# Order of the last slot-expert products, their part widths, and the last hidden slot in a fused attention and mixture-of-experts kernel

## The chip, the cores and the metric

The kernel runs on one core of one Trainium2 chip. The metric is the device time of one execution in microseconds. Three runs of the kernel before gave 500.28, 500.62 and 500.79 us; the median is 500.62. All data are float32 in memory.

## The reference

Three steps follow one another. Only the last one ends in the region of the change, but all three fix what it must compute.

```python
# attention: q, k, v (4, 8, 576, 64), p (4, 8, 32, 64)
p_packed = sm_attn(p, k, v)
x = sm_attn(q, p_packed, p_packed)        # -> (2304, 512)

# first mixture: 4 experts, w1 (512, 1024), w2 (1024, 512), probabilities per row
for e in range(4):
    h = np.maximum(x @ w1[e], 0.0)
    out += p[:, e:e + 1] * (h @ w2[e])
x = out

# second mixture: 8 experts with 4 slots each, m1 (512, 1024), m2 (1024, 512)
logits = x @ phi
d = softmax of logits over the rows
slot_input = (d.T @ x).reshape(8, 4, 512)
for e in range(8):
    h = np.maximum(slot_input[e] @ m1[e], 0.0)
    slot_out[e] = h @ m2[e]
c = softmax of logits over the slots
out = c @ slot_out.reshape(32, 512)       # (2304, 512)
```

## The kernel before, in words

**Main loop (L1057).** It runs over 128 slots `s`. A slot is 128 of an expert's hidden columns for one batch of 576 rows. `mm1(s)` (L614) multiplies on TensorE into two PSUM tiles `h`, one for each half of 288 rows. A half is evicted in one of two ways into `ht`: either ScalarE applies the relu (L637) and POOL (GpSimd) multiplies by the row's probability (L638), or VectorE does both in one instruction (L632). VectorE takes the second half of every odd slot, ScalarE with POOL the rest. `flip_h` (L643) then turns `ht` in blocks of 32 by 32 on VectorE into `hr` (L648); it is issued one slot later, ahead of the next slot's `mm1`. `logits` (L653) multiplies four slots' `ht` with `wphi` into `lg`, two PSUM banks.

**Between the loop and the stream.** After slot 127 the last `flip_h` and `logits` are issued, then the generator `softmaxes` (L689) is advanced step by step. Its first step copies `lg` to `la`, one half on ScalarE (L696) and one on VectorE (L697). Its second step sums over the four groups on TensorE (`lr`, L701) and reduces the result on VectorE (L707). The third step takes exponentials and turns them. `pooling` (L776) then multiplies the turned weights with `hr` into `pb` (L788).

**The stream.** From here on the matrices w2, m1 and m2 come in 80 chunks of 512 KB each (`chunks`, L821), all issued by SP in a fixed order (L863). A chunk goes to a slot of 128 by 1024 elements as soon as that slot is free: the slots are former buffers of the main loop, among them `wphi`, `work` and the regions of `hr`, which `pooling` sets free as it proceeds. TensorE works through the chunks in their order: products with w2 (`si`), with m1 (`hid`), and with m2 (`so`).

**m2 and the output.** `so_steps` (L816) lists 32 chunks of m2, each used by one turn of the loop at L1262. The products accumulate in one PSUM tile `so` of 512 columns. For the first five experts a chunk holds whole rows of 512 columns (two blocks of rows, four matmul records of 512 columns). The last three experts are cut into two column parts of 256 (`PARTS`): first all their chunks for columns 0 to 255, then all for columns 256 to 511. Such a chunk has four blocks of rows with 256 columns each (eight matmul records), and rows of 1 KB where a whole-width chunk has runs of 4 KB. When a part is complete, ScalarE copies it (L1282), TensorE sums over its four groups (`sr`, L1284), ScalarE changes the sign (`rr`, L1286), and 18 matmuls `o` (L1298) make the part's output in six tiles of three. The 18 results are evicted alternately by ScalarE and VectorE (`drain`, L1259), and SP stores each tile (L1305).

**What sets the order.** The program is written out by hand in this region: each engine executes its instructions in the order in which the code issues them. The `so` tile keeps one of six PSUM banks; `o` tiles rotate through the other five. A turn of the loop at L1262 that completes no part ends with `continue`, so the second part's products are issued after all of the first part's tiles.

Of the kernel before, what the change touches and what calls it, by code (L numbers as in the profile page):

```python
# [18 lines left out]
def tile_packed_attention_moe_softmoe(  # L19
# [21 lines left out]
    NB, H, S, D = q.shape  # L41
    NE, DM, DF = w1.shape
    NX = m1.shape[0]
# [6 lines left out]
    SPB = 4 * NCH  # L50
    NFT = DF // 128
# [3 lines left out]
    CHUNK = 1024  # L55
# [30 lines left out]
    def mm_ps(name, keep=False):  # L86
        i = min((i for i in range(6) if i not in kept), key=lambda i: idle_since[i])
        clock[0] += 1
        idle_since[i] = clock[0]
        t = bank(i, name)  # L90
        if keep:
            kept[i] = t
        return t
# [28 lines left out]
    def place(b, i):  # L122
        return (NE * b + i) % RING
# [488 lines left out]
    ht_t, hn_t, lg_t = {}, {}, {}  # L612

    def mm1(s):  # L614
        ci, kf = divmod(s, 4)
        b = ci // NCH
        gg = g_t[ci]
        pr = pe_t[ci // 2]
        ht = ht_pool.tile([128, S], F32, tag="ht", name=f"ht{s}")
        fs = slice(128 * kf, 128 * kf + 128)  # L620
        for r in range(2):
            ps = mm_ps(f"h{s}_{r}")
            ts = slice(HS * r, HS * r + HS)
            for g in range(2):
                ah, al = a2_t[b, g]
                for i, (l, m) in enumerate(((0, ah), (0, al), (1, ah))):
                    pe.matmul(  # L627
                        ps[:, :HS], gg[:, l, g, fs], m[:, ts],
                        start=(g == 0 and i == 0), stop=(g == 1 and i == 2),
                    )  # L630
            if r and kf % 2:
                dve.scalar_tensor_tensor(  # L632
                    out=ht[:, ts], in0=ps[:, :HS], scalar=0.0, in1=pr[:, ts],
                    op0=ALU.max, op1=ALU.mult,
                )
            else:
                act.activation(out=ht[:, ts], in_=ps[:, :HS], func=AF.Relu)  # L637
                pool.tensor_tensor(out=ht[:, ts], in0=ht[:, ts], in1=pr[:, ts], op=ALU.mult)  # L638
        ht_t[s] = ht
        if kf == 3:  # L640
            del g_t[ci]

    def flip_h(s):  # L643
        ci, kf = divmod(s, 4)
        b, ch = divmod(ci, NCH)
        i, hf = divmod(ch, 2)
        f0 = 32 * (4 * hf + kf)
        dve.transpose(  # L648
            out=hr[:, place(b, i), :, f0 : f0 + 32],
            in_=ht_t[s].rearrange("p (x t) -> p x t", t=32),  # L650
        )

    def logits(ci):  # L653
        b, ch = divmod(ci, NCH)
        e, hf = order[ci // 2], ci % 2
        if ch == 0:
            lg_t[b] = [bank(6 + r, f"lg{b}_{r}") for r in range(2)]
        for r in range(2):
            for x in range(4):
                pe.matmul(  # L660
                    lg_t[b][r][32 * x : 32 * x + 32, :HS],
                    wphi[:, NFT * e + 4 * hf + x, :],
                    ht_t[4 * ci + x][:, HS * r : HS * r + HS],
                    start=(ch == 0),
                    stop=(ch == NCH - 1),
                    tile_position=(0, 32 * x),
                )
        for x in range(4):
            del ht_t[4 * ci + x]
# [141 lines left out]
    parts, d0 = [], 0  # L811
# [1 line left out]
        parts.append((d0, dw))  # L813
        d0 += dw

    so_steps = [(i, x, 0, DM) for i in range(NX - 3) for x in range(0, NFT, CHUNK // DM)]  # L816
    for d0, dw in parts:
        so_steps += [
            (i, x, d0, dw) for i in range(NX - 3, NX) for x in range(0, NFT, CHUNK // dw)
        ]  # L820
    chunks = []  # L821
    for x in range(0, NFT, 2):
# [19 lines left out]
    def add_slots(n, make):  # L842

        group = []
        for i in range(n):
            slots.append((make, n, i, group))
# [47 lines left out]
    def leftover(p, n, k=0):  # L894
        return flat[p][:, left + k : left + k + n]
# [4 lines left out]
    with tc.manual_schedule():  # L900
# [118 lines left out]
        nslot = NB * SPB  # L1019
# [6 lines left out]
        sg = {}  # L1026
# [29 lines left out]

        for s in range(nslot):  # L1057
            ci, kf = divmod(s, 4)
            if s:
                flip_h(s - 1)  # L1060
            mm1(s)
            if kf == 0:
                if ci + 1 < NB * NCH:
                    for _ in make_g(ci + 1):
                        pass
                if ci:
                    while wphi_done[0] < min(ci, NCH):
                        next(wgen, None)
                    logits(ci - 1)
            if s < SPB:  # L1070
                for _ in range(2):
                    next(wgen, None)
            for f in todo.pop(s, []):
                f()
            for gen in list(att_gens):
                if next(gen, "end") == "end":
                    att_gens.remove(gen)
            last = s - (NB - 1) * SPB
            if last == 0:
                att.close()  # L1080
                open_stream("s1", "right")
                for _ in range(2):
                    add_slots(1, a2_place)
            elif last == 8:
                hr_slots([place(NB, 0)])
                fold = leftover(place(NB, 0), 64)
                pool.tensor_tensor(
                    out=fold.rearrange("p (a s) -> p a s", a=2),
                    in0=ident.rearrange("p (a b s) -> p a b s", a=2, b=2)[:, :, 0],
                    in1=ident.rearrange("p (a b s) -> p a b s", a=2, b=2)[:, :, 1],  # L1090
                    op=ALU.add,
                )
            elif last == SPB - 5:
                add_slots(2, w1_place)
                add_work(0)
                add_work(1)
            if last >= 0:
                fill_stream(1)
# [6 lines left out]


        b = NB - 1
        flip_h(nslot - 1)
        logits(NB * NCH - 1)
        sg[b] = softmaxes(b, True)  # L1110
        for _ in range(2):
            next(sg[b])
        wp = mm_ps("idle")
        for _ in range(20):
            pe.transpose(wp[:, :128], ident, ident)
# [47 lines left out]
        ck = 0  # L1163
# [95 lines left out]
            (act.copy if tn[0] % 2 else dve.tensor_copy)(dst, src)  # L1259

        so = mm_ps("so", keep=True)
        for n, (i, x, d0, dw) in enumerate(so_steps):  # L1262

            nx = CHUNK // dw
            t = chunk_t.pop(ck)
            ck += 1
            for xl in range(nx):
                c = (nx * n + xl) % 4
                pe.matmul(  # L1269
                    so[32 * c : 32 * c + 32, d0 : d0 + dw],  # L1270
                    hm[:, x + xl, 32 * i : 32 * i + 32],
                    t[:, dw * xl : dw * xl + dw],
                    start=(nx * n + xl < 4),
                    stop=(dw < DM and i == NX - 1 and x + nx == NFT),
                    skip_group_check=True,
                    tile_position=(0, 32 * c),
                )
            load_chunk()
            if dw == DM or i < NX - 1 or x + nx < NFT:
                continue  # L1280
            so_sb = leftover(1, dw, d0)
            act.copy(so_sb, so[:, d0 : d0 + dw])  # L1282
            sr = mm_ps(f"sr{d0}")
            pe.matmul(sr[:, :dw], rep, so_sb, start=True, stop=True)  # L1284
            rr = end[:, CHUNK : CHUNK + dw]
            act.mul(rr, sr[:, :dw], -1.0)  # L1286
            for b2 in range(NB // 2):
                rows = out[2 * b2 * S : 2 * (b2 + 1) * S, d0 : d0 + dw].rearrange(
                    "(r x) d -> r x d", x=XR
                )  # L1290
                cv = ct[:, b2].rearrange("p x b r t -> p x (b r t)")
                for j0 in range(0, XR, nt):
                    jn = min(XR - j0, nt)
                    ob = out_tile()
                    ps = [mm_ps(f"o{d0}_{b2}_{j0}_{j}", keep=True) for j in range(jn)]
                    for j in range(jn):
                        o = slice(32 * j, 32 * j + 32)
                        pe.matmul(  # L1298
                            ps[j][:, :dw], cv[o, j0 + j], rr[o], start=True, stop=True,
                            tile_position=(32 * j, 0),  # L1300
                        )
                    for j in range(jn):
                        drain(ob[:, dw * j : dw * j + dw], ps[j][:, :dw])
                    let_go(ps)
                    sp.dma_start(  # L1305
                        rows[:, j0 : j0 + jn, :],
                        ob[:, : dw * jn].rearrange("p (j d) -> p j d", d=dw),
                    )


# [28 lines left out]
```

## Time and profile before

| | us |
|---|---|
| median of three runs | 500.62 |
| the profiled execution | 500.28 |
| its span (first to last instruction) | 498.5 |
| TensorE matmul busy | 471.6 (95%) |
| VectorE busy | 295.4 (59%) |
| ScalarE busy | 182.9 (37%) |
| POOL busy | 198.0 (40%) |
| DMA, mean rate over the span | 209 GB/s, 104.35 MB |

Times in rows count from the start of the span. A record in the timeline begins with start and duration in us, then engine, line, operation, output and input. PE is TensorE's matmul, PEld its weight load, DVE is VectorE, ACT is ScalarE, SPq is SP's queue of instructions. Each float32 matmul leaves two records. The ends of matmuls are modelled. [...]

### The profile page before, as it was taken

What the parts mean: (1) busy time and instruction counts of PE and PEld (TensorE: products, weight loads), DVE (VectorE), ACT (ScalarE), POOL (GpSimd) and SP (SyncE); (2) the same over time, 40 slices, a digit from 0 to 9 for tenths busy, and PEclk for the clock granted to TensorE, in tenths of its full rate; (3) what the DMA queues carried; (4) which work ended last, traced back from release to release, by engine and by line L of the source; (5) the groups of instructions that cost most, each with busy time, mean ns of one, the idle gap of its engine ahead of it and who ended that gap; (6) DMA issues with size and microseconds to landing.
All of it is one profiled execution on the core that took longest, in us unless ns stands there. A gap on an engine that the chain in (4) does not pass through costs nothing.

```text
span 498.5 us, 13271 instructions
## 1 busy us (share of the span) xinstructions
PE 471.6 (95%) x5604; PEld 329.7 (66%) x5604; DVE 295.4 (59%) x556; ACT 182.9 (37%) x452; POOL 198.0 (40%) x251
## 2 busy tenths in 40 slices
PE   6888999999999999999999999999999999898694
PEld 3766877777675767788567787776787965331152
DVE  4682456687881778797458798872767632320022
ACT  1465555434440444445224344431434310110033
POOL 3023442356741445575325467642567602100000
PEclk9799999999999999999999999999999999899958
DMA  7989832755240355642224622393762689999995
GB/s 197 381 315 306 284 133 87 207 157 141 85 144 29 133 190 134 182 169 85 87 76 154 170 85 86 113 348 133 272 236 90 249 323 411 412 417 416 385 352 199
DMA packets 56203, 104.35 MB, mean 209 GB/s; under 512 B 5904, under 2 KB 22800, under 8 KB 56144
## 3 DMA queue, kind: packets, MB, share of 16 engines
q1 hardware_dynamic: 42816, 77.15, 44.7%
q10 hardware_dynamic: 13200, 26.22, 15.6%
q8 instruction: 44, 0.72, 0.6%
q0 software_dynamic: 128, 0.15, 0.2%
q14 instruction: 15, 0.12, 0.1%
HBM read 98.78 MB, written 4.72 MB: 208 GB/s over the span
## 4 chain that ended last, share of the span: by engine, by line
PE 69%; DMA 16%; DVE 8%; ACT 2%; SPq 2%; POOL 1%; issue 1%; DVEq 0%; ACTq 0%
PE h L627 35%; PE pb L788 8%; PE lg L660 6%; PE g L592 6%; DMA w<-in_moe_w_dram 4%; DMA hr<-in_moe_w_dram 4%; DMA ck<-in_moe_w_dram 4%; PE o L1298 2%; DMA work<-in_moe_w_dram 2%; PE pv L462 2%; DMA k<-in_k_dram 2%; PE sb L365 2%; PE w2t L262 2%; DVE hr L648 2%; DVE g L604 1%; DMA hr<-in_v_dram 1%
## 5 line engine op out<-in xcount | busy, mean ns | idle before, releaser
L638 POOL TENSOR_TENSOR ht<-ht,work 128x288 f32<-128x288 f32 x192 | 155.2, 818 | 176.2 <-ACT ht L637 175.9
L627 PE MATMUL h<-a,g 128*128 128x288 f32 x1536 | 224.5, 300 | 0.6 <-DVE a L549 0.6
L627 PEld LDWEIGHTS h<-a,g 128*128 128x128 f32 x1536 | 206.7, 188 | 26.8 <-issue 14.7
L637 ACT ACTIVATE ht<-h 128x288 f32<-128x288 f32 x192 | 78.8, 412 | 165.1 <-PE h L627 149.3
L648 DVE STREAM_TRANSPOSE hr<-ht 128x576 f32<-128x576 f32 x128 | 97.6, 763 | 39.5 <-POOL ht L638 36.8
L604 DVE TENSOR_TENSOR g<-g,g 128x512 fp32r<-128x512 f32 x64 | 41.2, 684 | 35.2 <-ACT g L602 35.2
L602 ACT CAST g<-g 128x512 fp32r<-128x512 f32 x64 | 34.5, 589 | 25.1 <-PE g L592 25.1
L632 DVE SCALAR_TENSOR_TENSOR ht<-h,work 128x288 f32<-128x288 f32 x64 | 28.1, 439 | 23.1 <-PE h L627 22.8
L660 PE MATMUL lg<-ht,wphi 128*32 128x288 f32 x512 | 39.2, 412 | 0.0
L592 PE MATMUL g<-w,pkn 64*32 64x512 f32 x512 | 34.9, 601 | 2.4 <-DMA w<-in_moe_w_dram 1.6
L660 PEld LDWEIGHTS lg<-ht,wphi 128*32 128x32 f32 x512 | 14.0, 109 | 33.6 <-POOL ht L638 23.8
L788 PE MATMUL pb<-hr,work 32*32 32x512 f32 x864 | 30.6, 598 | 0.0
L1259 DVE COPY ob<-o 128x256 f32<-128x256 f32 x9 | 3.6, 421 | 32.2 <-PE o L1298 32.2
L788 PEld LDWEIGHTS pb<-hr,work 32*32 32x32 f32 x864 | 12.6, 103 | 11.4 <-issue 8.7
L269 ACT COPY hr<-w2t 128x512 f32<-128x512 f32 x32 | 17.8, 597 | 6.2 <-PE w2t L262 6.1
L262 PE MATMUL w2t<-ident,hr 128*128 128x128 f32 x128 | 18.8, 287 | 0.2 <-ACT hr L269 0.2
L262 PEld LDWEIGHTS w2t<-ident,hr 128*128 128x128 f32 x128 | 15.1, 147 | 3.7 <-issue 1.2
L1269 PE MATMUL so<-hr 128*32 128x256 f32 (+1 forms) x84 | 12.6, 511 | 4.9 <-DMA hr<-in_moe_w_dram 4.7
L680 POOL COPY work<-dpn 128x576 f32<-128x576 f32 x16 | 10.9, 680 | 13.5 <-DVE dpn L196 13.5
L802 DVE SCALAR_TENSOR_TENSOR tacc<-tacc,rsc,pb 128x512 f32<-128x512 f32 x12 | 8.2, 742 | 13.4 <-PE pb L788 13.4
L1269 PE MATMUL so<-ck,hr 128*32 128x256 f32 (+1 forms) x80 | 12.2, 550 | 1.1 <-DMA ck<-in_moe_w_dram 1.1
L683 DVE STREAM_TRANSPOSE work<-work 128x576 f32<-128x576 f32 x16 | 12.2, 763 | 0.0
(180 smaller groups left out, 439.4 us busy)
## 6 DMA issues: line engine op xcount, KB each, us to landing
w<-in_moe_w_dram ACTq DMA_DIRECT2D x25, 1024.0 KB, 5.2
ck<-in_moe_w_dram SPq DMA_DIRECT2D x42, 512.0 KB, 8.3
hr<-in_moe_w_dram SPq DMA_DIRECT2D x32, 512.0 KB, 9.6
hr<-in_moe_w_dram SPq DMA_DIRECT2D x8, 1024.0 KB, 10.1
w<-in_moe_w_dram SPq DMA_DIRECT2D x7, 1024.0 KB, 5.6
k<-in_k_dram SPq DMA_DIRECT2D x16, 288.0 KB, 4.0
v<-in_v_dram SPq DMA_DIRECT2D x18, 192.0 KB, 5.3
q<-in_q_dram SPq DMA_DIRECT2D x12, 288.0 KB, 3.0
```

Source lines behind the costliest of these rows:

```text
L262: pe.transpose(st[x][:, 128 * dc : 128 * dc + 128], t[:, x, 128 * dc : 128 * dc + 128], ident,)
L592: pe.matmul(ps[g][c : c + 32, :], pkn_t[b][o : o + 64, g, hp, 0, :], t[o : o + 64, 2 * g + hp, :], start=True, stop=True, tile_position=(o ...
L602: act.copy(gg[:, 0, g], ps[g])
L604: dve.tensor_tensor(out=gg[:, 1, g], in0=ps[g], in1=gg[:, 0, g].bitcast(F32), op=ALU.subtract)
L627: pe.matmul(ps[:, :HS], gg[:, l, g, fs], m[:, ts], start=(g == 0 and i == 0), stop=(g == 1 and i == 2),)
L632: dve.scalar_tensor_tensor(out=ht[:, ts], in0=ps[:, :HS], scalar=0.0, in1=pr[:, ts], op0=ALU.max, op1=ALU.mult,)
L637: act.activation(out=ht[:, ts], in_=ps[:, :HS], func=AF.Relu)
L638: pool.tensor_tensor(out=ht[:, ts], in0=ht[:, ts], in1=pr[:, ts], op=ALU.mult)
L648: dve.transpose(out=hr[:, place(b, i), :, f0 : f0 + 32], in_=ht_t[s].rearrange("p (x t) -> p x t", t=32),)
L660: pe.matmul(lg_t[b][r][32 * x : 32 * x + 32, :HS], wphi[:, NFT * e + 4 * hf + x, :], ht_t[4 * ci + x][:, HS * r : HS * r + HS], start=(ch ...
L788: pe.matmul(pb[c][m : m + 32, :], d[o, x + par, :], hr[o, lo : hi + 1 : hi - lo, x + par, :], start=(x == 0), stop=(x == NBLK - 2), tile_p ...
L1269: pe.matmul(so[32 * c : 32 * c + 32, d0 : d0 + dw], hm[:, x + xl, 32 * i : 32 * i + 32], t[:, dw * xl : dw * xl + dw], start=(nx * n + xl ...
```

## The change

1. Two experts of m2 instead of three are loaded and multiplied in two column parts; six instead of five are loaded at whole width.
2. The loop over `so_steps` becomes a function that does one chunk. The first part is completed as before. Then its output tiles are issued, and after the second, third, fourth and fifth of the six tiles one chunk of the second part is multiplied. After the last tile what is left of them would follow. The second part's copy, sum, sign and tiles then follow at once.
3. In slot 127 VectorE evicts both halves of `h`. The turning of slot 126 is issued behind these evictions instead of ahead of slot 127's `mm1`. The turning of slot 127 is issued behind the first step of `softmaxes`, that is behind the copies of `lg` to `la`, instead of ahead of `logits`.

```diff
-            if r and kf % 2:
+            if (r and kf % 2) or s == NB * SPB - 1:
                 dve.scalar_tensor_tensor(
...
-    so_steps = [(i, x, 0, DM) for i in range(NX - 3) for x in range(0, NFT, CHUNK // DM)]
+    so_steps = [(i, x, 0, DM) for i in range(NX - 2) for x in range(0, NFT, CHUNK // DM)]
     for d0, dw in parts:
         so_steps += [
-            (i, x, d0, dw) for i in range(NX - 3, NX) for x in range(0, NFT, CHUNK // dw)
+            (i, x, d0, dw) for i in range(NX - 2, NX) for x in range(0, NFT, CHUNK // dw)
         ]
...
         for s in range(nslot):
             ci, kf = divmod(s, 4)
-            if s:
+            if s and s < nslot - 1:
                 flip_h(s - 1)
...
         b = NB - 1
-        flip_h(nslot - 1)
+        last_ht = ht_t[nslot - 1]
+        flip_h(nslot - 2)
         logits(NB * NCH - 1)
         sg[b] = softmaxes(b, True)
-        for _ in range(2):
-            next(sg[b])
+        next(sg[b])
+        ht_t[nslot - 1] = last_ht
+        flip_h(nslot - 1)
+        del ht_t[nslot - 1]
+        next(sg[b])
...
-        for n, (i, x, d0, dw) in enumerate(so_steps):
+        steps = enumerate(so_steps)
+
+        def slot_outputs():
+
+            nonlocal ck
+            n, (i, x, d0, dw) = next(steps)
...
             load_chunk()
-            if dw == DM or i < NX - 1 or x + nx < NFT:
-                continue
+            return dw < DM and i == NX - 1 and x + nx == NFT
+
+        for p, (d0, dw) in enumerate(parts):
+            ended = p > 0
+            while not ended:
+                ended = slot_outputs()
             so_sb = leftover(1, dw, d0)
             act.copy(so_sb, so[:, d0 : d0 + dw])
...
+                    if p == 0 and (b2 or j0):
+                        if ck < len(chunks):
+                            slot_outputs()
+            while p == 0 and ck < len(chunks):
+                slot_outputs()
```

## Rows read from the trace of the kernel before

**Rows 1.** The page's 40 slices: granted clock of TensorE in tenths.

```profile
PEclk9799999999999999999999999999999999899958
```

**Rows 2.** Chain of waits, 400 to 500 us: start, us, what.

```profile
464.39 8.09 DMA hr<-in_moe_w_dram
...
472.52 1.13 PE so L1269 x8
...
475.79 6.63 PE o L1298 x36
482.43 4.14 PE so L1269 x48
...
488.19 1.13 PE o L1298 x10
...
492.44 0.76 DVE work L1259 x2
```

**Rows 3.** Timeline, 448 to 474 us, TensorE's products with m2.

```profile
451.90 1.05 PE L1269 MATMUL so<-ck,hr 128*32 128x512 f32 x4 [0.23 <-DMA ck<-in_moe_w_dram]
...
458.15 1.05 PE L1269 MATMUL so<-hr 128*32 128x512 f32 x4 [0.17 <-DMA hr<-in_moe_w_dram]
...
465.71 0.64 PE L1269 MATMUL so<-hr 128*32 128x256 f32 x8 [0.34 <-DMA hr<-in_moe_w_dram]
...
472.52 1.08 PE L1269 MATMUL so<-hr 128*32 128x256 f32 x8 [0.58 <-DMA hr<-in_moe_w_dram]
```

**Rows 4.** Windows: busy of PE, PEld, DVE, ACT, POOL; granted clock, DMA share, GB/s.

```profile
460.00:462.00 2.00, 1.64 (x9) 0.32 (x8) 0.00 (x0) 0.00 (x0) 0.00 (x0) 1.00 1.03 419
...
470.00:472.00 2.00, 1.16 (x16) 0.16 (x8) 0.00 (x0) 0.00 (x0) 0.00 (x0) 0.88 1.09 386
...
474.00:475.00 1.00, 0.90 (x2) 0.50 (x2) 0.00 (x0) 0.04 (x1) 0.00 (x0) 0.50 1.09 347
...
480.00:481.00 1.00, 1.00 (x10) 0.74 (x7) 0.52 (x2) 0.55 (x3) 0.00 (x0) 0.50 1.04 351
...
485.00:486.00 1.00, 1.00 (x24) 0.57 (x20) 0.00 (x0) 0.00 (x0) 0.00 (x0) 0.92 0.92 320
```

**Rows 5.** Timeline, 470 to 500 us: an eviction, the second part's products and tiles.

```profile
482.23 0.37 ACT L1259 COPY hr<-o 128x256 f32<-128x256 f32 x1 [0.46 <-DMA out_dram<-ob]
...
482.79 0.20 PEld L1269 LDWEIGHTS so<-ck,hr 128*32 128x32 f32 x4 [0.23 <-issue]
483.21 0.20 PEld L1269 LDWEIGHTS so<-ck,hr 128*32 128x32 f32 x4 [0.23 <-issue]
...
488.19 4.55 PE L1298 MATMUL o<-work,hr 32*128 32x256 f32 x36 [0.47 <-ACT work L1286]
```

**Rows 6.** Timeline, 388 to 422 us: the last slots and what follows.

```profile
393.63 5.04 PE L627 MATMUL h<-a,g 128*128 128x288 f32 x36
...
396.80 2.40 POOL L638 TENSOR_TENSOR ht<-ht,work 128x288 f32<-128x288 f32 x3 [0.79 <-ACT ht L637]
...
398.44 0.78 DVE L648 STREAM_TRANSPOSE hr<-ht 128x576 f32<-128x576 f32 x1 [1.57 <-POOL ht L638]
...
398.60 1.81 PE L660 MATMUL lg<-ht,wphi 128*32 128x288 f32 x16
399.14 0.42 DVE L632 SCALAR_TENSOR_TENSOR ht<-h,work 128x288 f32<-128x288 f32 x1
...
400.45 0.46 DVE L697 COPY la<-lg 128x288 f32<-128x288 f32 x1
...
401.21 1.00 DVE L707 TENSOR_REDUCE lmx<-lr 128x1 f32<-128x288 f32 x2 [0.30 <-PE lr L701]
...
403.83 9.85 PE L788 MATMUL pb<-hr,t 32*32 32x512 f32 x288
```

**Rows 7.** Timeline of SP's queue, 385 to 500 us.

```profile
406.17 9.18 SPq L863 DMA_DIRECT2D hr<-in_moe_w_dram  x12
```

**Rows 8.** Line 1305, the output stores: time to landing.

```profile
DMA to landing us min/median/max: 2.4/4.2/4.9
```

## The prediction

> **What bounds the kernel now.** I read the 40 slices first: TensorE's granted clock stands at 9 or more in nearly all of them, but at 5 in the slice before the last [rows 1]. That is the place to look at. Then the chain of waits for the last 35 us [rows 2]: until 472.5 it is transfers of m2, so the stage is bound by the DMA stream; from 472.52 it is TensorE with short evictions: the first part's last products with m2 (`so`), their sum and sign (sr, rr), the first part's output tiles (`o`), all the second part's products, and the second part's tiles. Third, the timeline of L1269 shows how far apart the chunks of m2 land: whole-width ones 1.25 us ((458.15 - 451.90) / 5), half-width ones 1.362 us ((472.52 - 465.71) / 5) [rows 3]. Fourth, the windows: the clock falls from 1.00 to 0.50 inside 470 to 472 (0.88 there, so near 471.8), and comes back inside 485 to 486 (0.92, so near 485.1) [rows 4]. So the first part's tiles and most of the second part's products run at 1.2 GHz, and the second part's tiles at 2.4 GHz.
>
> The profiled execution took 500.28 us, 1.78 more than its span of 498.5. It is the lowest of three runs whose median is 500.62. I work out a difference against the profiled execution and put it on the median.
>
> **Edit 1, two experts in parts instead of three.** The first part is now complete with 24 whole chunks and 4 halves (28) instead of 20 and 6 (26). The stream is saturated before (419 GB/s in 460 to 462, 386 with halves in 470 to 472 [rows 4]), so the last of them lands 4 x 1.25 - 2 x 1.362 = 2.28 us later. The first part's products then end at 473.65 + 2.28 = 475.93. The half-width chunks also begin 5.0 us later, and the clock's fall, which came 6.1 us after the first of them, may come later too. If it falls only after 476.8, the sum and sign run at 2.4 GHz and the way from the last product to the first tile takes 1.62 us as in the second part (486.57 to 488.19) instead of 2.14 (473.65 to 475.79) [rows 2]. I take 2.14, the row of the same place, since four sparse chunks still precede it, and keep -0.5 us for the range. First tile: 478.07.
>
> [...] The rows differ: 1.25 against 1.362, and so the delay is the 2.28 above.
>
> **Edit 2, products among tiles.** Before, six tiles and six chunks' products stood one after another from 475.79 to 486.57, 10.78 us [rows 2]. Now two tiles, then four times (one chunk's products, one tile). The two chunks less are the two that the first part now has to wait for.
> - A tile of three matmuls costs 6.63 / 6 = 1.10 us at 1.2 GHz [rows 2] and 4.55 / 6 = 0.76 at 2.4 GHz [rows 5].
> - A chunk's eight records cost 0.85 us at 1.2 GHz (four every 0.425, from 482.79 to 483.21 [rows 5]), an estimate of 0.43 at twice the clock.
> - A pair of both is at most 1.95 at the lower clock. At least it is 1.70: the tile's two passes of 256 columns should need no more than the chunk's, and what the tile has beyond is waiting for evictions, which the chunk's products can cover. I take 1.85. At the higher clock the ends are 1.19 and 0.86; I take 1.05.
>
> All at 1.2 GHz: 2 x 1.10 + 4 x 1.85 = 9.60 us. All pairs at 2.4 GHz: 2.20 + 4 x 1.05 = 6.40. The trace of before has no such alternation, so the clock is the unknown. From 476 to 482 the tiles alone kept PE's busy share at 1.00 and the clock stayed at 0.50 [rows 4]; it came back 2.7 us into the dense products. I take its return at the same time as before, 485.1, since by then the engine has done both kinds for 5 us. From 480.27 (after two tiles) to 485.1 are 4.83 / 1.85 = 2.6 pairs, the other 1.4 take 1.47. The stretch ends at 486.57, in 8.5 us.
>
> Do the chunks land in time? At 347 GB/s (474 to 475 [rows 4]) a half chunk takes 1.51 us, so the four land at 476.3, 477.8, 479.3 and 480.8; they are wanted at 480.3, 482.1, 484.0 and 485.3. That is 4 us of slack, of which the first two output stores (128 x 768 x 4 bytes, 1.13 us each at that rate) can take 2.3 from the last. No wait in front of a tile. On SP's queue all loads are issued ahead of the first output store, as before.
>
> What is late next: ScalarE. The second part's copy of `so` now stands in its queue behind the eviction of the sixth tile, one copy of 0.37 us [rows 5] that TensorE's last tile must end before; earlier, the six products lay between. With the handover 0.4 us. Then sum and sign at 2.4 GHz, 1.62 us. The second part's first tile starts at 486.57 + 0.4 + 1.62 = 488.59 against 488.19: +0.40 us. From there all is as before: six tiles and six stores, 10.31 us to the end of the span.
>
> **Edit 3, the last slot.** Removed: one ScalarE eviction and one multiplication on POOL, the last of a run of three at 0.80 us that ends at 399.20; `lg` waits for it [rows 6]. Added: a second eviction on VectorE (0.42). Moved: the last two turnings by VectorE (0.78 each), the first behind both evictions, the second behind the copy of `la`. In the new order VectorE's queue is: eviction of the second half, possible when `h` ends at 398.67, to 399.12; turning to 399.90; `lg` is ready 0.85 after that eviction (the old distance, 399.56 to 400.41), 399.97; copy of `la` 400.01 to 400.47; turning to 401.25; then the reduction, which started at 401.21 [rows 6]. So `lg` is ready 0.44 us earlier, and VectorE is late next, with the same work in another order: +0.04, I take 0. Ends: -0.44 if the turning found a gap, +0.42 if the added eviction counted in full. What the reduction releases is the pooling at 403.83, and its progress lets SP issue the stream's twelve transfers from 406.17 on [rows 6, 7]; a shift there moves the whole stream, and a shift of `lg` alone does not.
>
> **Sum.** Edit 1 +2.28, edit 2 -10.78 + 8.50 = -2.28, the eviction in front of the copy +0.40, edit 3 0: +0.40 us. 500.28 + 0.4 = 500.7 by the profiled execution, 501.0 by the median.
>
> **Rivals.**
> - *Slower: the clock does not come back among the mixed instructions.* For it: tiles alone did not raise it. Against: half of the work is now of the kind that did. The stretch takes 9.60 (478.07 to 487.67), then 0.4 and 2.14: tiles from 490.21, and these at 1.10 instead of 0.76. Their evictions end near 490.21 + 6.63 + 0.4 = 497.2. The span ends between 499.6, since a store took 2.4 us at the least [rows 8], and 502.5, since 5.3 us lay behind the last eviction before (493.20 [rows 2]), which followed faster tiles; I take the middle, 501.1: +2.6, 503.2. It decides from the point where the clock has not risen when the sixth tile ends; each microsecond of a later rise costs about 0.45.
> - *Faster: the clock rises with the first pair or does not fall before the tiles.* With all pairs at 2.4 GHz the stretch takes 6.40, the second part's tiles start at 486.5: -1.7, 498.9. Were the clock never to fall, the sum from the last chunk of the first part (474.80) is 0.64 [rows 3] + 1.62 + 2 x 0.76 + 4 x 1.05 + 0.4 + 1.62, tiles from 484.80: -3.4, 497.2. For it: the alternation leaves TensorE no idle time. [...]
> - *The last slot does gain.* The reduction starts 0.44 earlier, and with it the stream: 500.6.
> - *A chunk holds a tile.* If the second part's loads come more than 2 us later still, the tiles behind wait on TensorE's queue: +1, 502.
>
> **How the numbers follow.** Forecast 0.42, with its own range of 500.2 to 502 (the pair between 1.70 and 1.95, the clock's return a microsecond or two off, edit 1's -0.5, edit 3's ends); clock not back 0.25; clock early 0.22; last slot 0.07; chunk late 0.04. With 0.2% (1.0 us, about what a measurement of this kernel can tell from no change): of the forecast 0.31 same, 0.09 slower, 0.02 faster; clock not back 0.25 slower; early 0.19 faster, 0.03 same; last slot 0.06 and 0.01 faster; late chunk 0.02 and 0.02 slower. Faster 0.22, same 0.42, slower 0.36. The range reaches to both clock cases: 498.9 to 503.2.
>
> **What would show it.** Of the changed kernel: the last half chunk of the first part starts on TensorE near 474.8; the first tile near 478.1; `so` of 8 records between tiles two to six, none waiting for a DMA; the second part's copy of `so` behind a ScalarE eviction; the reduction L707 at 401.2; SP's twelve transfers from 406.2. The prediction is wrong if the stretch from the first tile to the second part's copy differs from 8.9 us by more than one, which the granted clock there would explain, or if the stream itself is shifted.

## The result and the profile after

The changed kernel took 507.39 us in the median of four runs (507.0 to 508.28); the kernel before took 500.71 beside it (500.28 to 503.29). The ratio is 1.0125, 95% interval 1.0088 to 1.0162: slower, outside the range on record. Both kernels measured again gave 507.33 against 501.61, ratio 1.0106 (1.0065 to 1.0146). Single times of the kernel before ranged from 498.58 to 504.93 in one set of 31 executions, far more than the 0.5 us that the first three showed.

The page's granted clock shows the place at once. It ended in 9, 5, 8 before [rows 1]; now it ends in 5, 5:

```profile
PEclk9599999999999999999999999999999999999955
```

The chain of waits of the changed kernel (start, us, what) has the new order, one chunk's products between tiles, and behind it a sum and tiles that take longer than the second part's before; the sign takes 0.39 us in both:

```profile
479.53 2.89 PE o L1311 x12
482.43 1.01 PE so L1278 x8
483.44 1.16 PE o L1311 x6
484.60 1.01 PE so L1278 x8
...
489.96 1.25 PE o L1311 x6
491.21 0.35 ACT hr L1263
491.56 0.28 ACT hr L1295
...
491.89 1.24 PE sr L1297 x2
...
493.58 6.32 PE o L1311 x34
```

The same places in the kernel before; its tiles began at 488.19 [rows 2]:

```profile
487.01 0.71 PE sr L1284 x2
...
489.34 3.08 PE o L1298 x20
```

Its windows (columns as in [rows 4]) say why. By their records, whose ends are modelled, TensorE's matmuls are busy without a gap from 480 to 491, and yet the clock stays at 0.50 to the end:

```profile
480.00:482.00 2.00, 2.00 (x12) 1.21 (x9) 0.78 (x2) 0.96 (x3) 0.00 (x0) 0.50 0.55 176
...
486.00:488.00 2.00, 2.00 (x17) 0.54 (x17) 0.76 (x2) 0.37 (x1) 0.00 (x0) 0.50 0.58 197
...
494.00:496.00 2.00, 2.00 (x15) 1.51 (x13) 0.74 (x2) 0.92 (x3) 0.00 (x0) 0.50 0.00 1
```

The two spans differ by 6.8 us (498.5 and 505.3). Cut at the same events, with the times of the rows (the second part's copy starts at 491.45 by the timeline; the chain lists it only from 491.56, where the eviction ahead of it ends):

| stretch | before | after | difference | forecast |
|---|---|---|---|---|
| start to the end of `h` | 398.67 | 400.16 | +1.49 | 0 |
| end of `h` to the first tile | 77.12 | 79.37 | +2.25 | +2.28 |
| first tile to the second part's copy | 10.80 | 11.92 | +1.12 | -1.88 |
| copy to the second part's first tile | 1.60 | 2.13 | +0.53 | 0 |
| second part's first tile to the end | 10.31 | 11.72 | +1.41 | 0 |

```profile
491.45 0.38 ACT L1295 COPY hr<-so 128x256 f32<-128x256 f32 x1
```

The first line is no work of the change. It arises before any instruction that the change touches. In part it comes from the start, where the clock was low for longer: 13.65 us (13.58 to 27.23) instead of 6.83 (14.13 to 20.95). This is the window of 22 to 24 us, first of the kernel before, then of the changed one:

```profile
22.00:24.00 2.00, 2.00 (x81) 1.82 (x82) 1.38 (x4) 0.83 (x4) 0.00 (x0) 1.00 1.05 409
```

```profile
22.00:24.00 2.00, 2.00 (x34) 1.68 (x34) 1.51 (x4) 0.75 (x2) 0.00 (x0) 0.50 1.05 409
```

About half of the 1.49 is left of that when the loop has run for a while (0.81 at 329.75). The other half arises between 337 and 344 us, where the same 96 records of the pooling (L788) take 4.08 us instead of 3.40; the clock stood at 1.00 in both, and the cause was not found. In profiles of five other kernels of this study, equal in their instructions up to the last slot, the last product L592 before it began between 1.1 us earlier and 2.2 us later than in the profile of before. So of the 6.8, some 5.3 lie behind that point, where the change is.

### The profile page after: what moved, and what is told of

The parts are those of the page before. It is cut to its first block, busy times and chain, and to the rows that moved or that the text cites. A ratio compares the mean times of both kernels' runs of the same rounds, so it can differ in the third digit from the quotient of the medians.

```text
span 505.3 us, 13235 instructions
## 1 busy us (share of the span) xinstructions
PE 480.2 (95%) x5588; PEld 332.0 (66%) x5588; DVE 295.4 (58%) x557; ACT 182.3 (36%) x451; POOL 197.1 (39%) x250
## 4 chain that ended last, share of the span: by engine, by line
PE 67%; DMA 17%; DVE 9%; ACT 2%; SPq 1%; POOL 1%; issue 1%; ACTq 0%
PE h L627 34%; DMA hr<-in_moe_w_dram 7%; PE pb L788 7%; DMA ck<-in_moe_w_dram 6%; PE lg L660 6%; PE g L592 6%; PE pv L462 3%; PE o L1311 3%; PE sb L365 2%; DMA w<-in_moe_w_dram 2%; PE w2t L262 2%; PE sa L365 2%; DVE hr L648 2%; DVE g L604 1%; DMA p<-in_p_dram 1%; PE et L426 1%
## 5 line engine op out<-in xcount | busy, mean ns | idle before, releaser
L592 PE MATMUL g<-w,pkn 64*32 64x512 f32 x512 | 34.9, 601 | 0.4 <-DMA w<-in_moe_w_dram 0.4
L788 PE MATMUL pb<-hr,work 32*32 32x512 f32 x864 | 31.3, 598 | 0.0
L788 PEld LDWEIGHTS pb<-hr,work 32*32 32x32 f32 x864 | 12.7, 103 | 12.0 <-issue 9.3
L1278 PE MATMUL so<-hr 128*32 128x512 f32 (+1 forms) x68 | 13.7, 553 | 3.2 <-DMA hr<-in_moe_w_dram 3.0
L1278 PE MATMUL so<-ck,hr 128*32 128x256 f32 (+1 forms) x80 | 13.8, 573 | 3.1 <-DMA ck<-in_moe_w_dram 3.1
L1311 PE MATMUL o<-work,hr 32*128 32x256 f32 x72 | 14.5, 688 | 0.9 <-ACT work L1299 0.9
```

Source lines behind the costliest of these rows:

```text
L592: pe.matmul(ps[g][c : c + 32, :], pkn_t[b][o : o + 64, g, hp, 0, :], t[o : o + 64, 2 * g + hp, :], start=True, stop=True, tile_position=(o ...
L788: pe.matmul(pb[c][m : m + 32, :], d[o, x + par, :], hr[o, lo : hi + 1 : hi - lo, x + par, :], start=(x == 0), stop=(x == NBLK - 2), tile_p ...
L1311: pe.matmul(ps[j][:, :dw], cv[o, j0 + j], rr[o], start=True, stop=True, tile_position=(32 * j, 0),)
```

## The experiments

Theory A: the loss is in the tail, where TensorE's clock doesn't come back because products and tiles alternate. Rivals: B, the last slot costs; C, the clock stays low because there are fewer products, whatever their order; D, the clock is a by-product and the switch between products and tiles, with the later first part, takes the time. The runs come from three chips; each ratio is against the kernel before on the same chip.

**The last slot alone.** On the kernel before, only the edits of slot 127:

```diff
-            if r and kf % 2:
+            if (r and kf % 2) or s == NB * SPB - 1:
...
-            if s:
+            if s and s < nslot - 1:
                 flip_h(s - 1)
...
```

> The kernel before with the last-slot edit alone (VectorE evicts both halves of slot 127, turnings behind). Theory A (the whole loss is in the tail: the clock stays at 1.2 GHz among the mixed instructions): this edit is harmless, in the changed kernel's trace the pooling began 4.66 us after the end of h against 5.16, so 0 to 0.5 us faster, 500.2 to 500.7, clock back at full speed before the second part's tiles. Theory B (the last slot costs, since h ended 1.5 us later in the changed kernel's trace): about 1.5 us slower, 502.

Measured: 502.43 us (500.49 to 503.66) against 501.68, ratio 1.0015 (0.9986 to 1.0044). No change that can be told; a cost of 1.5 us would be a ratio of 1.003, which lies inside the interval.

**The change without the last slot.** The converse: that edit taken back.

> The changed kernel without its last-slot edit. Theory A: nearly all of the loss stays, 506.5 to 508, granted clock 0.50 from the first tile to the end. Theory B: 1.5 us of the loss goes, 505.5.

Measured: 506.31 against 501.68, ratio 1.0087 (1.0050 to 1.0124). From the first tile (480.67) to the second part's first tile (494.72) are 14.05 us, as in the changed kernel (479.53 to 493.58), and the clock is 0.50 throughout:

```profile
480.67 2.89 PE o L1307 x12
...
494.72 6.32 PE o L1307 x34
```

The loss in the tail doesn't need the last slot. The median lies between what A and B expected, so by itself it doesn't say whether the last slot costs something besides; two runs further down, the kernel before kept busy with and without that edit, differ by 0.04 us, and with them B falls.

**Two experts in parts alone.** The order of products and tiles is that of before.

```diff
-    so_steps = [(i, x, 0, DM) for i in range(NX - 3) for x in range(0, NFT, CHUNK // DM)]
+    so_steps = [(i, x, 0, DM) for i in range(NX - 2) for x in range(0, NFT, CHUNK // DM)]
...
-            (i, x, d0, dw) for i in range(NX - 3, NX) for x in range(0, NFT, CHUNK // dw)
+            (i, x, d0, dw) for i in range(NX - 2, NX) for x in range(0, NFT, CHUNK // dw)
```

> The kernel before with two experts of m2 in parts instead of three, order of tiles and products as before. First tile 2.3 us later, then six tiles (6.6) and four chunks' products in one block (3.4 at 1.2 GHz). Theory A (dense products bring the clock back, alternation does not): clock at 1.00 before the second part's tiles as before, about +0.9 us: 501.5. Rival C (what matters is how long the products last, whatever their order; four chunks are too few): clock stays at 0.50, sum and second tiles slow: +0.9 +0.5 +1.4, 503.5 or more.

Measured: 502.07 against 501.68, ratio 1.0020 (0.9993 to 1.0047). The chain has six tiles, then four chunks in one block, then a sum at the higher clock (0.71):

```profile
478.56 6.63 PE o L1298 x36
485.19 3.17 PE so L1269 x32
...
488.81 0.71 PE sr L1284 x2
...
489.98 1.13 PE o L1298 x10
```

And the windows, in which the clock rises during the block (0.57 is the mean of a window that it leaves at 1.00):

```profile
486.00:488.00 2.00, 2.00 (x28) 0.91 (x20) 0.00 (x0) 0.00 (x0) 0.00 (x0) 0.57 1.08 369
488.00:490.00 2.00, 1.02 (x13) 0.32 (x5) 0.00 (x0) 0.76 (x2) 0.00 (x0) 1.00 0.30 99
```

Tiles and products are as many as in the changed kernel, and the clock is back. C falls. Against the run without the last slot only edit 2, the order, differs: 506.31 and 502.07 us, measured side by side, so the order by itself cost 4.2 us.

**The changed kernel kept busy.** Idle turnings of the identity, whose result nobody uses, fill TensorE's waits behind the first part's half-width chunks and around sum and sign:

```diff
+        def stay(k):
+            wp = mm_ps("idle")
+            for _ in range(k):
+                pe.transpose(wp[:, :128], ident, ident)
...
             load_chunk()
+            if dw < DM and d0 == 0:
+                stay(5)
             return dw < DM and i == NX - 1 and x + nx == NFT
...
             act.copy(so_sb, so[:, d0 : d0 + dw])
+            if p:
+                stay(4)
...
             act.mul(rr, sr[:, :dw], -1.0)
+            stay(4)
```

> The changed kernel with idle turnings of the identity on TensorE (result unused): five behind each half-width chunk of the first part, four in each wait for sum and sign. Theory A: clock 1.00 through the tail; first tile 0.5 us earlier, the stretch to the second part's copy 6.4 to 7.2 us instead of 11.9, sum and sign 0.5 less, second tiles and stores 1.4 less: 499 to 501. Rival D (the clock is a by-product, the time goes into the switch between products and tiles and the later first part): clock at 1.00 yet 504 or more.

Measured: 499.84 against 501.68, ratio 0.9969 (0.9938 to 1.0000). Chain and window:

```profile
478.00 1.13 PE o L1322 x10
...
479.85 0.57 PE so L1284 x8
480.42 0.64 PE o L1322 x6
...
486.61 1.13 PE o L1322 x10
```

```profile
478.00:482.00 4.00, 3.98 (x40) 1.90 (x40) 1.67 (x4) 1.57 (x5) 0.00 (x0) 1.00 0.76 246
```

From first tile to second part's first tile 8.61 us instead of 14.05, a pair 1.21 instead of 2.17. The change lost its time to the clock; D as the main cause falls. The second tiles and stores gave back less than expected: 10.69 us to the end, not 10.31. No run shows why: the second part's tiles ran at the same clock in the kernel before.

**The changed kernel again**, beside the next three:

> The changed kernel itself, beside the others on one chip. Theory A (the clock stays at 1.2 GHz from the first part's tiles to the end because products alternate with tiles): 506 to 508, granted clock 0.50 from the first tile on, pair of one chunk and one tile 2.17 us. If some executions show the clock back at full speed, single times near 502 to 504 are among them.

Measured: 507.33 (505.27 to 509.63). First tile 481.02, second part's 495.07, again 14.05 us, pair 2.17, clock 0.50 to the end. No single time was near 502 to 504.

**All four chunks in one block behind the second tile.**

```diff
                     if p == 0 and (b2 or j0):
-                        if ck < len(chunks):
+                        while ck < len(chunks):
                             slot_outputs()
```

> The changed kernel with the second part's four chunks in one block behind the second tile instead of one behind each of tiles two to five; all else equal. Theory A (dense products bring the clock back, alternation does not): the clock returns during or just after the block (3.4 us at 1.2 GHz), the last four tiles or at least the second part run at 2.4 GHz: 3 us or more faster than the changed kernel, 502 to 504. Rival C (the first part's tiles so close to the end keep the clock low whatever the order): as the changed kernel, 506 to 508.

Measured: 504.20 (502.43 to 505.43) against 501.61, ratio 1.0038 (1.0011 to 1.0064). The chain, then the windows:

```profile
480.96 2.89 PE o L1311 x12
483.86 3.02 PE so L1278 x32
486.88 1.06 PE o L1311 x10
...
490.61 0.71 PE sr L1297 x2
```

```profile
484.00:486.00 2.00, 2.00 (x24) 0.87 (x20) 0.32 (x1) 0.00 (x0) 0.00 (x0) 0.50 0.86 290
486.00:488.00 2.00, 1.98 (x27) 0.97 (x19) 0.42 (x2) 0.46 (x2) 0.00 (x0) 0.95 0.24 79
...
492.00:494.00 2.00, 1.98 (x17) 1.53 (x16) 0.81 (x2) 0.92 (x3) 0.00 (x0) 0.75 0.86 302
```

The clock is back at 486.2, before the block ends, and five matmuls of tiles then take 1.06 us. It is lost again: behind the waits around the second part's sum it falls near 493.0 (the 0.75 of the last window), and most of the second part's tiles run at 0.50. So this order keeps only a part of what the block gained. The distance between the two first tiles is 10.82 us, 3.2 less than with single chunks, and the medians differ by 3.1. Nothing but the place of the products was changed. Nor does the clock come back by itself a set time after its fall: it was low for 13.7 us in the kernel before (471.5 to 485.2), for 10.2 us here (476.0 to 486.2), and from 477.8 to the end, over 27 us, in the changed kernel.

**Two chunks behind the second tile, two behind the fourth.**

```diff
+                    ob_n[0] += 1
                     if p == 0 and (b2 or j0):
-                        if ck < len(chunks):
+                        for _ in range(2 * (ob_n[0] in (2, 4))):
                             slot_outputs()
```

> The changed kernel with two chunks behind the second tile and two behind the fourth, instead of one behind each of tiles two to five. One chunk at a time left the clock at 0.50 to the end (two profiles of the changed kernel and one without the last slot); four in a block brought it back within 3 us. Theory A (it is the run of products without tiles between that counts): if two are enough, clock back before the second part's tiles and near the block of four, 504; if not, 0.50 to the end, but two switches fewer at 0.16 us or so each: 506 to 507.

Measured: 508.30 against 500.87, ratio 1.0126 (1.0092 to 1.0160). Two in a row did not bring it back: no row of the tail shows another clock than 0.50. The time lies above what either case expected. The chain:

```profile
483.75 1.87 PE so L1279 x16
485.62 2.83 PE o L1312 x12
488.44 1.87 PE so L1279 x16
490.31 2.82 PE o L1312 x12
```

The expected gain of the fewer switches was not to be seen either: 13.92 us between the two first tiles against 14.05.

**Kept busy, with products behind all six tiles.** As the kept-busy kernel above, without the alternation.

> The changed kernel kept busy, with the second part's four chunks behind all six tiles, as the kernel before had its six. At a clock of 1.00 a pair took 1.21 us (0.57 and 0.64), a tile alone is 0.76 and a chunk alone 0.43 to 0.46, so 1.19 to 1.22: if the alternation costs only through the clock, equal to the changed kernel kept busy (499.8), stretch of 6.4 to 6.6 us against 6.66; if its switches cost by themselves, up to 1 us faster.

Measured: 499.25 against 500.87, ratio 0.9967 (0.9947 to 0.9988). Between the two first tiles 8.07 us (478.09 to 486.16), so 0.54 less than with alternation. The chain's tiles and products:

```profile
479.24 3.39 PE o L1322 x22
482.63 1.86 PE so L1284 x32
```

In these two profiles the alternation costs half a microsecond at a clock of 1.00, but not in the pairs: a tile (4.52 / 6) and a chunk (1.86 / 4) take 1.22 together, a pair took 1.21. Of the 0.54, 0.35 lie in the stretch, with its first two tiles, which took 1.85 (479.85 - 478.00) instead of two times 0.75, and 0.19 behind the last tile, at the eviction in front of the copy. The ratios of the two (0.9969 and 0.9967) can't tell them apart.

**The kernel before kept busy.** The same idle turnings in the kernel before.

> The kernel before with idle turnings of the identity on TensorE in the same places (five behind each half-width chunk of the first part, four in the waits for sum and sign; result unused). Theory A: clock 1.00 through the tail; tiles 0.76 each and chunks 0.43 to 0.57 each, 7.2 to 8 us instead of 10.8, sum and sign of the first part 0.5 less: 3 to 4 us faster than before, and, its first part being 2.3 us earlier, 1 to 2 us faster than the changed kernel kept busy (499.84). If loads of the second part then hold TensorE, less: the wait shows at the products.

Measured: 497.64 (496.63 to 498.78) against 501.61, ratio 0.9915 (0.9878 to 0.9953), faster than both. Its chain:

```profile
477.22 3.39 PE o L1309 x22
480.61 2.73 PE so L1275 x48
...
485.00 1.13 PE o L1309 x10
```

Between the two first tiles 8.94 us; it was 12.40 before. The first part starts 2 us earlier than in the kernels with two experts in parts, and that outweighs the two chunks more.

**The same with the last slot.**

> The same with the last-slot edit as well. In the traces that edit let the pooling begin 0.4 to 0.5 us sooner after the end of h, while its own time was not told from no change (ratio 1.0015). If the stream's start carries it to the end: up to 0.5 us faster than the same without it; if the stream makes up for it or the difference drowns in the spread of the times: equal.

Measured: 497.68, ratio 0.9912 (0.9880 to 0.9944). From the end of `h` to the first tile 76.81 us, without the last slot 76.80.

**Idle turnings at the start too.** Eight more behind the first sixteen, nine behind the second group's first scores.

> The kernel before with the last-slot edit and the tail kept busy, and now with idle turnings also in two waits of the first 14 us (eight more behind the first sixteen, nine behind the second group's first scores). In every profile so far the clock fell to 0.50 somewhere in 7 to 17 us and came back between 11 and 27 us, with the first h of the loop between 36.95 and 39.80. If that spread is the clock's, h starts at 37 or sooner, the times spread less, and the median is 1 to 2 us under 497.7; if idle turnings there only delay the scores, equal or slower.

Measured: 497.94 (496.47 to 498.99), ratio 0.9924 (0.9896 to 0.9952): no gain over 497.68. The clock still fell, near 16.4 us, and the first `h` of the loop began at 37.91. This expectation was wrong; what ends the low stretch near the start stays open.

The tails side by side, from the profiles (us; the second column counts from the first part's first tile):

| kernel | clock in the tail | to the second part's first tile | from there to the end |
|---|---|---|---|
| before | back at 485.2 | 12.40 | 10.31 |
| changed, single chunks | 0.50 to the end | 14.05 | 11.72 |
| blocks of two | 0.50 to the end | 13.92 | 11.72 |
| one block of four | back at 486.2, lost again at 493.0 | 10.82 | 11.12 |
| block behind all tiles | back at 487.7 | 11.42 | 10.32 |
| changed, kept busy | 1.00 | 8.61 | 10.69 |
| kept busy, block behind all tiles | 1.00 | 8.07 | 10.64 |
| before, kept busy | 1.00 | 8.94 | 10.90 |

## Why the prediction was wrong

**The step that failed** is in edit 2: "I take its return at the same time as before, 485.1, since by then the engine has done both kinds for 5 us." It did not return at all. The clock before came back in a block of six chunks' products [rows 4, 5], and I put that down to the kind of work. The runs show that it is the unbroken block: four in a row (3.17 us behind all tiles, 3.02 behind the second) brought it back, two and two (1.87 each) or four single ones (1.01 each) did not, although every tile and product is the same and the matmul busy share is 2.00 of 2.00 in each window of the alternating tails from 482 to 490. Why the alternating stream does not bring the clock back, no run shows. The row of tiles alone [rows 4] had already said that a full busy share isn't enough, and I read it as a property of tiles. The clock's fall was read wrongly too, though nothing hung on it: 0.88 in 470 to 472 puts it at 471.5, not 471.8.

**The pair and the first two tiles were mis-sized.** I held 1.70 to 1.95 us and took 1.85; it was 2.17 at a clock of 0.50 and 1.21 at 1.00 (held: 0.86 to 1.19). I wrote 1.2 and 2.4 GHz for these two clocks; no run shows a frequency, the profile gives the clock as a share of full speed. I had assumed that what a tile takes beyond a chunk's 0.85 is waiting for evictions, which products would cover. In the new order the evictions are indeed covered, yet at 0.50 the weight loads stand idle at each of the four switches to a chunk, 0.65 us, and back to a tile, 0.81. The timeline of the changed kernel, with TensorE's matmuls, its weight loads and what they idled for:

```profile
482.36 0.20 PEld L1278 LDWEIGHTS so<-ck,hr 128*32 128x32 f32 x8 [0.65 <-issue]
482.36 1.08 PE L1278 MATMUL so<-ck,hr 128*32 128x256 f32 x8
482.47 0.42 DVE L1263 COPY ob<-o 128x256 f32<-128x256 f32 x1 [0.40 <-PE o L1311]
483.37 0.51 PEld L1311 LDWEIGHTS o<-work,hr 32*128 32x128 f32 x6 [0.81 <-DVE ob L1263]
```

A chunk behind a tile takes 1.01 us instead of 0.85, a tile behind a chunk 1.16 instead of 1.10, so neither hides in the other. The eviction that the row of the tile's loads names (DVE) had ended at 482.89, 0.48 us before them; what did end as they began is the chunk (482.36 + 1.08 = 483.44, a modelled end). Whether the loads had to wait for it, no run shows.

The first two tiles were put at 2.20, twice the mean of six in a row; they took 2.89, and two tiles standing by themselves took 2.82 to 2.89 in the run with blocks of two as well. With the measured pairs and first two tiles, and the clock back at 485.1, the stretch would have been 2.89 + 4.14 + 2.09 x 1.21 = 9.6 us, so these errors are worth 1.1 over the 8.5, and the missing clock 2.1 more of the 11.7 that it took until TensorE's last tile ended.

**The slower rival was the one that happened**, at 0.25. Its time of 503.2 was too low: its stretch took 11.68 instead of 9.60 (+1.3 by the four pairs, +0.7 by the first two tiles), its last tiles to the end took 11.72 where I had 10.9, and the start added 1.49 that has nothing to do with it. The sum and sign at the lower clock (2.13 with the copy, 2.14 there) and the eviction in front of the copy (0.35 from 491.21, 0.4 there) were as worked out.

**Edit 1 came out right in part by luck**: first tile 2.25 us later, forecast 2.28. The row of the last half chunk shows two misses that nearly cancel:

```profile
476.71 0.68 PE so L1278 x8
```

Counted from the end of `h` it started 2.70 us later than before, not 2.28; the half chunks started 1.33, 1.53 and 1.50 us apart, not 1.362. But its products took 0.68 instead of 1.13, since the clock fell only at 477.8, behind them. That is later than the 476.8 from which I expected a faster sum, and still the sum, from 477.84, ran at the lower clock. In the other seven profiles of kernels with two experts in parts the distance from `h` to the first tile was 79.5 to 81.1 us where the changed kernel had 79.37, and in the one with the last slot alone 78.4 against 77.12. These differences of the stream from run to run were not resolved, so the direction and about the size of the delay are shown, the match to 0.03 us is not. No `so` between tiles waited for a transfer, as forecast.

**Edit 3 was half right.** `lg` was ready 1.22 us after the end of `h` instead of 1.74, 0.52 sooner where I had 0.44. The reduction did not stay where it was: it began 2.32 us after `h` instead of 2.54. The timeline of the changed kernel:

```profile
395.11 5.05 PE L627 MATMUL h<-a,g 128*128 128x288 f32 x36
...
400.08 1.29 PE L660 MATMUL lg<-ht,wphi 128*32 128x288 f32 x16
400.19 0.46 DVE L632 SCALAR_TENSOR_TENSOR ht<-h,work 128x288 f32<-128x288 f32 x1 [0.35 <-PE h L627]
400.57 0.77 DVE L648 STREAM_TRANSPOSE hr<-ht 128x576 f32<-128x576 f32 x1
...
401.79 0.77 DVE L648 STREAM_TRANSPOSE hr<-ht 128x576 f32<-128x576 f32 x1
...
402.48 0.78 DVE L707 TENSOR_REDUCE lmx<-lr 128x1 f32<-128x288 f32 x2
...
404.82 9.78 PE L788 MATMUL pb<-hr,t 32*32 32x512 f32 x288
```

VectorE's instructions follow each other with less than their full durations between starts (the turning 0.38 us after an eviction of 0.46), and both reductions now run without the wait between them (0.78 together, 1.00 in [rows 6]). The pooling begins 4.66 us after `h` instead of 5.16. That is a little beyond the outer bound of 0.44 that I gave, and it did not reach the first tile (76.81 against 76.80 with the tail kept busy). What takes it up in the stream was not settled.

**The range was too narrow for a second reason.** I took 0.2% for what a measurement can tell. The start alone moved by 1.49 us between the two profiles, and the kernel before by 6 us between executions.

## What to carry to other kernels

Where the clock is low, ask what brought it back and keep that piece whole: spreading a dense block of matmuls among others can cost more than the waits it fills (here 4.2 us), though the busy share looks perfect (2.00 of 2.00). Before reordering a tail that runs at the lower clock, try to keep it from falling: some forty idle matmuls in waits that exist anyway were worth 4 us here, and the changed kernel, kept busy too, stayed behind that (499.84 against 497.64). A profile of one execution and three times say little on a kernel whose clock differs from run to run (mean granted clock 0.953 to 0.984 in 31 executions of the kernel before).

## What the hardware showed

- With a matmul busy share of 1.00, by modelled ends, the granted clock stayed at 0.50 for 11 us (480 to 491) among alternating tiles and products; one block of four chunks, 3.02 us, brought it back.
- Idle turnings kept the clock: with five behind each sparse chunk and four in each wait it stood at 1.00 in every window from 470 to 489 in the five kernels kept busy, where the changed kernel without them had 0.50 from 477.8 on. The trace records them as matmuls (idle<-ident, 128x128); the runs show them holding the clock among other matmuls, not raising it.
- Near the start, the same instructions saw the clock fall and return at different times in different executions (low from 14.1 to 21.0 us in one profile, 13.6 to 27.2 in another).
